# An attention, MLP and mixture-of-experts chain on one core: eight weight conversions moved, and the gates' end interleaved with early expert blocks

## Chip, cores and metric

The kernel runs on one core of one Trainium2 chip. The metric is the device time of one execution in microseconds (us); lower is better.

## What is computed

Three layers follow one another. The output of each is the next one's input.

```python
def _attn_ref(q, k, v, f):                      # 4 batches, 8 heads, 576 positions, 64 wide
    scores = q @ k.T / sqrt(D)                  # per batch and head
    cum = cumsum(log(clip(f, 1e-4, 1)))
    scores = where(causal, -1e9, scores + cum[i] - cum[j])
    return softmax(scores) @ v

def _moe_ref(x, w_in, w_out):                   # 2304 tokens, 512 -> 2048 -> 512
    h = x @ w_in
    return (h * clip(h + 3, 0, 6) / 6) @ w_out

def _moe2_ref(x, w_gate, w_output_gate, w1, w2):   # 8 experts, 512 -> 1024 -> 512
    logits = x @ w_gate
    e_idx = argmax(logits, axis=1)              # one expert for each token
    gate_w = softmax(logits)[e_idx]
    eom = sigmoid(x @ w_output_gate)
    for e in range(8):
        mask = e_idx == e
        out[mask] = gate_w * eom[mask, e] * (relu(x[mask] @ w1[e]) @ w2[e])
```

All of it is float32. The kernel splits each float32 operand into a high half (fp16) and a low half (bf16) and makes each product of three matmuls: high by high, high by low, low by high.

## The kernel before

**Attention** (`attn_seq`) is a long generator of steps: loads and transposes of q, k and v, score matmuls (L295), a softmax on VectorE, ScalarE and GpSimd, and the products with v (L428 to L443). At the end of each group of tokens VectorE scales the result (`xs`, L453), GpSimd makes its low half (`xn`, L457), and SyncE's DMA queue transposes it into `xT` (L491), the input of the MLP.

**The MLP** (`moe1_steps`) takes the 2304 tokens in 6 chunks of 384. A chunk has 16 up-products of 12 matmuls (L695), each evacuated by ScalarE (`hr`, L699) and VectorE (L702) and split (L703, L707), and then 4 down-products of 48 matmuls (L718), evacuated to `x2` (L727, L728). The steps of attention for later tokens are issued between the MLP's steps, so that TensorE has work of both.

**Weight conversion.** `w_in` and `w_out` come as 16 raw tiles each (`load_raw`), and `conv_raw` turns a tile into its halves by a route that keeps the low bits: three integer instructions on VectorE (L658, L660, L662), a copy on ScalarE (L665) and a subtraction (L666) on GpSimd, or on VectorE for two in three of `w_out`'s. `EARLY_CONV` says how many of the 32 tiles are converted among attention's steps before the first chunk; the rest are converted in the first chunk's steps, one for each of its first six steps and then two. Where a conversion is issued in the program is not yet where it runs: a scheduler orders the instructions by priorities, and the conversions in the chunk's steps stand under `high_priority(offset=CONV_FIRST)`, 500, against attention's 200. SP, the engine that issues most loads, has its order by hand there.

**Gates** (`gate_steps(c)`, three parts divided by `yield`). Part one: 36 matmuls (L783) for the logits of a chunk's three token tiles, and the tokens' rows transposed (L791) and stored to DRAM (`rows`, L793, on GpSimd's queue). Part two: a chain on VectorE from `lg` (L797) to the one-hot of the chosen expert (`oh`, L805) and running sums of it (`ohsum`, L809), six small matmuls (L814, L815) that rank each token within its expert (`rank`, L824), the gate's value in three pieces (L816 to L836), and `M` (L837), the values spread over the experts. Gates of chunks 0 to 4 run inside the next chunk's steps. The last chunk's run after its last down-product.

**Count and table.** `count_rounds` counts the tokens of each expert (one matmul, L889, and five VectorE instructions, L892 to L896) for the loop at the end. `rank_onehot` writes `R`, a one-hot of each token's rank (L938). `table` multiplies `R` by `M` (18 token tiles by 2 blocks, 36 matmuls, L916), so that for each slot of each expert it gives the token's row number and gate value (L920 to L929). GpSimd then gathers rows by these numbers (L950), SyncE transposes them into `xs` (L953), and each expert runs `expert1` (8 groups of 12 matmuls, L976, evacuated by ScalarE, L979, and VectorE, L980) and `expert2` (24 matmuls a block, L995, scaled on ScalarE, L1001, and scattered on GpSimd's queue, L1002).

**Early blocks.** The first 128 slots of experts 0 and 1 are filled from the first five chunks' tokens alone, by a table of their own (`R0`, L1126) made during the last chunk. Their `expert1` (`first`, one generator for each, 16 groups in all) and `expert2` run before the main blocks. They read and write room in `wi`, and their sums are in `ps_mm`, a PSUM pool of 3 buffers. From here on the order of PE, ScalarE and VectorE is the program's own (`manual_schedule`):

```python
for g_ in gq:                 # last chunk's gates, all of them
    for _ in g_: pass
count_rounds()
run(first[0], 2)              # two groups of expert 0's early block
rank_onehot x 3; table(R, ...)
rest of first[0], first[1]; expert2 of both; main blocks
```

Of the kernel before, what the change touches and what calls it, by code (L numbers as in the profile page):

```python
# [43 lines left out]

WO_STEP = 12

EARLY_CONV, EARLY_LOADS = 18, 21

PE_PIECES = 4

# [8 lines left out]
def attention_moe_kernel(ctx: ExitStack, tc: tile.TileContext, q, k, v, f, w_in, w_out,  # L59
# [713 lines left out]
    def gate_steps(c):  # L773
# [34 lines left out]
        for i in range(n):  # L808
            nc.vector.tensor_tensor(out=ohsum[:, f0 + i + 1], in0=ohsum[:, f0 + i], in1=oh[:, f0 + i],  # L809
                                    op=ALU.add)  # L810
        pr = ps_mm.tile([P, 512], F32, tag="mm", name="mm")
        for i in range(n):
            o = pr[:, i * E:(i + 1) * E]
# [72 lines left out]
    def count_rounds():  # L886

        ps = ps_mm.tile([P, 512], F32, tag="mm", name="mm")
        nc.tensor.matmul(ps[:, 0:E], lhsT=allone, rhs=ohsum[:, NB], start=True, stop=True)  # L889
        mx = mp2.tile([P, 1], F32, tag="cmx", name="cmx")  # L890
        more = mp2.tile([P, 8], F32, tag="more", name="more")
        nc.vector.tensor_reduce(out=mx, in_=ps[:, 0:E], axis=AX.X, op=ALU.max)  # L892
        nc.vector.tensor_tensor(out=more, in0=mx.to_broadcast([P, 8]), in1=thr, op=ALU.is_gt)
        nc.vector.tensor_reduce(out=mx, in_=more, axis=AX.X, op=ALU.add)
        nc.vector.tensor_copy(out=nrounds, in_=mx)
        nc.vector.tensor_copy(out=cnt, in_=ps[:, 0:E])  # L896
# [40 lines left out]
    def rank_onehot(R, i, s0, s1):  # L937
        nc.vector.tensor_scalar(out=R[:, i], in0=iota[:, s0:s1], scalar1=rank[:, i:i + 1], scalar2=None,  # L938
                                op0=ALU.is_equal)
# [23 lines left out]
    def expert1(e, ps_pool, blocks):  # L963

        W1, (xs, o) = wts[e, 0], xs_t[e, blocks[0]]
        hT, ho = h_t[e, blocks[0]]
        w = len(blocks) * P
        hs = slice(ho, ho + w)
        for m in range(F2 // P):
            ps = ps_pool.tile([P, 512], F32, tag="mm", name="mm")  # L970
            i = 0
            for j in range(KD):
                for a, b2 in ((0, 0), (0, 1), (1, 0)):
                    l = W1[:, a, j, m * P:(m + 1) * P]
                    r = xs[:, b2 * KD + j, o:o + w]
                    nc.tensor.matmul(ps[:, 0:w], lhsT=l.bitcast(BF16) if a else l, rhs=r.bitcast(BF16) if b2 else r,  # L976
                                     start=i == 0, stop=i == 3 * KD - 1)
                    i += 1
            nc.scalar.activation(out=hT[:, m, 0, hs], in_=ps[:, 0:w], func=AF.Relu)  # L979
            nc.vector.scalar_tensor_tensor(out=hT[:, m, 1, hs].bitcast(BF16), in0=ps[:, 0:w], scalar=0.0,  # L980
                                           in1=hT[:, m, 0, hs], op0=ALU.max, op1=ALU.subtract)
            yield
# [93 lines left out]
    for c in range(NCH):  # L1076
# [56 lines left out]
            while len(complete) < need[c + 1]:  # L1133
                adv()
        gq.append(gate_steps(c))
    for g_ in gq:
        for _ in g_:
            pass
    run(wg_, 4 * KD + 1 - nw)
    count_rounds()  # L1140
    ET = mybir.EngineType

    first = [expert1(e, ps_mm, (0,)) for e in range(2)]
    manual = ctx.enter_context(ExitStack())
    manual.enter_context(tc.manual_schedule(engines={ET.PE, ET.Activation, ET.DVE}))
    run(first[0], 2)
    for i in range(NBL, NB):
        rank_onehot(R, i, P, CAP)
    table(R, P, const, ps_mm, (1, 2), NB)
    for g_ in first:  # L1150
        run(g_, F2 // P)
# [2 lines left out]
            pass  # L1154
    moe1_ctx.close()
    xp = ctx.enter_context(tc.tile_pool(name="xp", bufs=1))
    ps2 = ctx.enter_context(tc.tile_pool(name="ps2", bufs=5, space=PSUM))
    regs = []

    def round_(first):  # L1160
# [85 lines left out]
```

## Time and profile before

| | |
|---|---|
| median of 3 runs | 831.59 us (827.8 to 831.8) |
| the profiled execution's own time | 830.41 us |
| its span, first to last instruction | 828.7 us |
| mean granted TensorE clock | 0.964 of full speed |
| TensorE busy (matmuls) | 744.0 us, 90% of the span |
| VectorE, ScalarE, GpSimd busy | 470.3, 449.9, 317.2 us |

The busy shares are means over stages that differ. The stage of attention alone takes the first 70 us or so; attention and the MLP share the engines up to some 580 us; the gates' end, the table and the early blocks lie between 588 and 619 us; the main blocks fill the rest. A row of a timeline gives the start, the duration and the instruction, and in brackets how long its engine stood idle just before it and what ended that.

### The profile page before, as it was taken

Reading aid. Unit: us, or ns where it says so; the run is one execution under the profiler, and the core shown is the slowest. Engines: PE = TensorE matmul, PEld = TensorE weight load, DVE = VectorE, ACT = ScalarE, POOL = GpSimd, SP = SyncE. Lnnn points to the kernel's source line nnn. Section 1 sums busy time; section 2 is a strip of 40 time slices with the busy share of each in tenths; the row PEclk is TensorE's granted clock in tenths of the full one; section 3 lists DMA queues with packets and bytes.
Section 4 is the critical chain, followed back from the end, with each engine's and each line's share of the span. In section 5 each row is a group of like instructions: output and inputs, shape, how many; then the busy total and the mean of one; then the engine's idle time right before and its main releaser. Section 6 shows DMA issues by size and latency. Waiting matters only on the chain.

```text
span 828.7 us, 16710 instructions
## 1 busy us (share of the span) xinstructions
PE 744.0 (90%) x6177; PEld 478.4 (58%) x6177; DVE 470.3 (57%) x1267; ACT 449.9 (54%) x909; POOL 317.2 (38%) x393
## 2 busy tenths in 40 slices
PE   4745989978899999998999999999899999999993
PEld 2533556645655655565665666566668665667641
DVE  7998988547651865158623776760313555554510
ACT  4864789756882775277724654550113545454510
POOL 9546788845753463145522500000131232310010
PEclk9986989989999999998999999999999999999997
DMA  8758799979985783497623847612474899895410
GB/s 248 214 184 192 180 214 257 193 128 167 176 154 116 138 141 74 74 145 143 107 55 67 145 138 238 177 41 51 78 150 94 240 281 267 231 265 200 149 37 29
DMA packets 263778, 127.95 MB, mean 154 GB/s; under 512 B 214658, under 2 KB 247522, under 8 KB 263684
## 3 DMA queue, kind: packets, MB, share of 16 engines
q1 hardware_dynamic: 251860, 105.20, 58.5%
q0 software_dynamic: 4960, 15.73, 5.5%
q10 hardware_dynamic: 6864, 5.80, 2.6%
q8 instruction: 54, 0.88, 0.4%
q14 instruction: 40, 0.33, 0.1%
HBM read 71.52 MB, written 10.08 MB: 98 GB/s over the span
## 4 chain that ended last, share of the span: by engine, by line
PE 38%; DMA 28%; DVE 11%; issue 7%; ACT 7%; POOL 4%; SPq 2%; ACTq 0%; another core or an unknown queue 0%; POOLq 0%; DVEq 0%
PE mm L718 14%; PE mm L695 12%; DMA out_dram<-y,ids 7%; DMA stw<-in_moe_w_dram 4%; DMA xg<-rows,ids 4%; PE mm L976 4%; DMA pt<-pn 3%; PE mm L995 3%; PE sc L295 2%; DMA q<-qp 2%; DMA K<-kp 2%; DVE W L879 1%; ACT ms L376 1%; DMA ldk<-in_k_dram 1%; DVE g L707 1%
## 5 line engine op out<-in xcount | busy, mean ns | idle before, releaser
L695 PE MATMUL mm<-xT,wi 128*128 128x384 f16 (+1 forms) x1152 | 213.3, 335 | 7.5 <-DMA xT<-xn 5.1
L718 PE MATMUL mm<-g,wo 128*128 128x384 f16 (+1 forms) x1152 | 199.8, 326 | 1.9 <-ACT g L703 1.1
L695 PEld LDWEIGHTS <-wi 128*128 128x128 f16 (+1 forms) x1152 | 112.1, 100 | 85.2 <-issue 19.7
L718 PEld LDWEIGHTS <-wo 128*128 128x128 f16 (+1 forms) x1152 | 110.7, 98 | 75.2 <-issue 4.6
L976 PEld LDWEIGHTS <-W 128*128 128x128 f16 (+1 forms) x1344 | 100.6, 99 | 16.2 <-issue 8.0
L879 DVE TENSOR_TENSOR W<-stw,W 128x1024 bf16<-128x1024 f32 x64 | 77.7, 1224 | 52.8 <-ACT W L878 48.8
L376 ACT ACTIVATE ms<-ms,nm 128x512 f32<-128x512 f32 (+4 forms) x144 | 78.8, 576 | 48.5 <-DVE nm L342 27.1
L394 POOL TENSOR_TENSOR pn<-ms,pn 128x384 bf16<-128x384 f32 (+1 forms) x80 | 82.4, 1034 | 57.8 <-ACT pn L393 52.6
L976 PE MATMUL mm<-xs,W 128*128 128x256 f16 (+3 forms) x1152 | 97.1, 246 | 4.7 <-DVE hT L980 2.3
L995 PE MATMUL mm<-W,hT 128*128 128x512 f16 (+1 forms) x432 | 94.4, 379 | 1.0 <-DVE hT L980 0.6
L878 ACT ACTIVATE W<-stw 128x1024 f16<-128x1024 f32 x64 | 66.9, 1054 | 47.7 <-DMA stw<-in_moe_w_dram 45.4
L707 DVE TENSOR_TENSOR g<-hr,g 128x384 bf16<-128x384 f32 x80 | 58.1, 726 | 33.6 <-ACT g L703 33.4
L342 DVE CUSTOM_DVE_ANT_1 ms<-sc,mask 128x128 f32<-128x128 f32 (+3 forms) x128 | 59.2, 486 | 26.1 <-PE sc L295 12.1
L995 PEld LDWEIGHTS <-hT 128*128 128x128 f16 (+1 forms) x432 | 41.9, 98 | 51.3 <-issue 1.9
L702 DVE SCALAR_TENSOR_TENSOR hr<-hr,mm 128x384 f32<-128x384 f32 x96 | 52.7, 549 | 28.1 <-ACT hr L699 27.5
L703 ACT ACTIVATE g<-hr 128x384 f16<-128x384 f32 x96 | 49.4, 515 | 28.0 <-DVE hr L702 27.4
L699 ACT ACTIVATE hr<-mm,bias 128x384 f32<-128x384 f32 x96 | 54.4, 567 | 16.5 <-PE mm L695 14.5
L980 DVE SCALAR_TENSOR_TENSOR hT<-mm,hT 128x128 bf16<-128x128 f32 (+1 forms) x96 | 32.0, 355 | 50.4 <-ACT hT L979 48.1
L428 PE MATMUL pv<-vt,pt 128*128 128x65 f16 x320 | 41.2, 198 | 20.9 <-DVE xs L453 9.4
L1002 POOL DMA_INDIRECT out_dram<-y,ids x18 | 20.7, 1148 | 97.9 <-ACT y L1001 57.2
L295 PE MATMUL sc<-K,q 128*128 128x256 f16 (+3 forms) x192 | 48.7, 296 | 6.4 <-DVE nm L342 4.3
L393 ACT ACTIVATE pn<-ms 128x384 f16<-128x384 f32 (+1 forms) x80 | 44.3, 556 | 13.3 <-DMA pt<-pn 12.9
(189 smaller groups left out, 1113.5 us busy)
## 6 DMA issues: line engine op xcount, KB each, us to landing
stw<-in_moe_w_dram SPq DMA_DIRECT2D x64, 512.0 KB
wo<-in_moe_w_in_dram SPq DMA_DIRECT2D x16, 512.0 KB
raw<-in_moe_w_out_dram ACTq DMA_DIRECT2D x11, 512.0 KB
rows<-rw POOLq DMA_DIRECT2D x15, 256.0 KB, 3.5
ldk<-in_k_dram SPq DMA_DIRECT2D x14, 256.0 KB
ldq<-in_q_dram SPq DMA_DIRECT2D x14, 256.0 KB
ldv<-in_v_dram SPq DMA_DIRECT2D x13, 256.0 KB
g<-in_moe_w_out_dram SPq DMA_DIRECT2D x3, 512.0 KB
```

The source lines that it names most:

```text
L295: nc.tensor.matmul(po, lhsT=lhs[0:rows], rhs=r if n > 1 else r[:, :, 0], start=x == 0, stop=x == 1)
L342: nc.vector.tensor_tensor_reduce(out=pairs(ms[:, off:off + w]), in0=ps[:, 0:w].rearrange("p (c j) -> p c j", c=2), in1=pairs(mask[:, 640 - ...
L376: nc.scalar.activation(out=ms[:, off:off + w], in_=ms[:, off:off + w], func=AF.Exp, scale=-1.0, bias=nm[:, i:i + 1])
L394: nc.gpsimd.tensor_tensor(out=lo.bitcast(BF16), in0=ms[:, 0:N], in1=hi, op=ALU.subtract)
L695: nc.tensor.matmul(ps[:, 0:w], lhsT=l.bitcast(BF16) if a else l, rhs=r.bitcast(BF16) if b2 else r, start=i == 0, stop=i == 3 * KD - 1)
L699: nc.scalar.activation(out=hr, in_=ps[:, 0:w], func=AF.Relu, bias=bias3)
L707: either.tensor_tensor(out=g[:, m, 1, 0:w].bitcast(BF16), in0=hr, in1=g[:, m, 0, 0:w], op=ALU.subtract)
L718: nc.tensor.matmul(ps[:, 0:w], lhsT=l.bitcast(BF16) if a else l, rhs=r.bitcast(BF16) if b2 else r, start=i == 0, stop=i == 3 * NF - 1)
L878: nc.scalar.activation(out=hi, in_=sts[i], func=AF.Copy)
L879: nc.vector.tensor_tensor(out=lo.bitcast(BF16), in0=sts[i], in1=hi, op=ALU.subtract)
L976: nc.tensor.matmul(ps[:, 0:w], lhsT=l.bitcast(BF16) if a else l, rhs=r.bitcast(BF16) if b2 else r, start=i == 0, stop=i == 3 * KD - 1)
L995: nc.tensor.matmul(ps, lhsT=l.bitcast(BF16) if a else l, rhs=r.bitcast(BF16) if b2 else r, start=i == 0, stop=i == 3 * NF2 - 1)
```

## The change

It has two parts.

1. `EARLY_CONV` goes from 18 to 10: eight tiles' conversions (and the room they free for later raw loads) are issued in the first chunk's steps rather than ahead of it.
2. At the gates' end a third `yield` splits part two of `gate_steps` ahead of the ranking matmuls. The last chunk's gates are no longer run as one piece. The order becomes: two groups of the early block; the logits and VectorE's chain up to `ohsum`; three groups; the ranking, the gate's values and `M`; the count; three `R`; three groups of expert 0 and two of expert 1; the table; the remaining six groups; `expert2`. The early blocks' sums go to `ps2`, a pool of 5 PSUM buffers that was opened later before, and the manual order begins earlier.

Lines below L810 are one further down in the changed kernel (L814 is now L815, L976 is L977), and those of the expert stage's caller up to four.

```diff
-EARLY_CONV, EARLY_LOADS = 18, 21
+EARLY_CONV, EARLY_LOADS = 10, 21
...
             nc.vector.tensor_tensor(out=ohsum[:, f0 + i + 1], in0=ohsum[:, f0 + i], in1=oh[:, f0 + i],
                                     op=ALU.add)
+        yield
         pr = ps_mm.tile([P, 512], F32, tag="mm", name="mm")
...
-    for g_ in gq:
-        for _ in g_:
-            pass
     run(wg_, 4 * KD + 1 - nw)
-    count_rounds()
     ET = mybir.EngineType
-
-    first = [expert1(e, ps_mm, (0,)) for e in range(2)]
+    ps2 = ctx.enter_context(tc.tile_pool(name="ps2", bufs=5, space=PSUM))
+
+    first = [expert1(e, ps2, (0,)) for e in range(2)]
     manual = ctx.enter_context(ExitStack())
     manual.enter_context(tc.manual_schedule(engines={ET.PE, ET.Activation, ET.DVE}))
+    last, = gq
     run(first[0], 2)
+    run(last, 2)
+    run(first[0], 3)
+    run(last, 2)
+    count_rounds()
     for i in range(NBL, NB):
         rank_onehot(R, i, P, CAP)
+    run(first[0], 3)
+    run(first[1], 2)
     table(R, P, const, ps_mm, (1, 2), NB)
     for g_ in first:
         run(g_, F2 // P)
...
-    ps2 = ctx.enter_context(tc.tile_pool(name="ps2", bufs=5, space=PSUM))
```

Three places in the engines' orders show what this does. The first is GpSimd (POOL) ahead of the first chunk, where L457 is the low half of attention's result (`xn`) and L666 the low half of a converted weight tile. Before:

```order
L666 TENSOR_TENSOR wi<-w_588,wi 128x4x128
L457 TENSOR_TENSOR xn<-xs,xn 128x128
L666 TENSOR_TENSOR wi<-w_622,wi 128x4x128
L666 TENSOR_TENSOR wi<-w_665,wi 128x4x128
L457 TENSOR_TENSOR xn<-xs,xn 128x128
L666 TENSOR_TENSOR wi<-w_700,wi 128x4x128
```

and with the change:

```order
L666 TENSOR_TENSOR wi<-w_923,wi 128x4x128
L457 TENSOR_TENSOR xn<-xs,xn 128x128
L666 TENSOR_TENSOR wi<-w_948,wi 128x4x128
L457 TENSOR_TENSOR xn<-xs,xn 128x128
L666 TENSOR_TENSOR wi<-w_973,wi 128x4x128
L666 TENSOR_TENSOR wi<-w_1018,wi 128x4x128
```

One conversion now stands between the last two `xn` where two stood. On VectorE likewise 12 conversions instead of 13 are done ahead of the last `xs` (L453) of the first chunk, and 16 instead of 17 ahead of the first `hr` (L702); the others, though written later, are placed by their priority where they were. On TensorE 116 of attention's score matmuls (L295) stand ahead of the first chunk's last up-product, where 129 stood, and 188 in both cases ahead of the second chunk.

The second place is VectorE at the gates' end. L837 (now L838) is the end of the gates' chain, L938 (L939) the table's one-hot `R`, L980 (L981) an early block's evacuation, L920 to L924 (L921 to L925) the table's results. Before:

```order
L836 TENSOR_TENSOR vals<-z,vb 128x3
L980 SCALAR_TENSOR_TENSOR wi<-mm,wi 128x128
L938 TENSOR_SCALAR R<-iota,rank 128x256 x2
L837 TENSOR_TENSOR M<-vals,oh 128x168
L938 TENSOR_SCALAR R<-iota,rank 128x256
L920 COPY sv<-mm 128x112
L922 SCALAR_TENSOR_TENSOR u<-sv 128x16
L924 CAST ids<-u 128x16
```

and with the change:

```order
L838 TENSOR_TENSOR M<-vals,oh 128x168
L893 TENSOR_REDUCE cmx<-mm 128x1
L894 TENSOR_TENSOR more<-cmx,thr 128x8
L895 TENSOR_REDUCE cmx<-more 128x1
L896 CAST nrounds<-cmx 128x1
L897 CAST cnt<-mm 128x8
L939 TENSOR_SCALAR R<-iota,rank 128x256 x3
L981 SCALAR_TENSOR_TENSOR wi<-mm,wi 128x128 x5
L921 COPY sv<-mm 128x112
L923 SCALAR_TENSOR_TENSOR u<-sv 128x16
L925 CAST ids<-u 128x16
```

The count has moved behind `M`, and five evacuations stand ahead of the table's results. The third place is ScalarE in the same stretch; L727 is the last evacuation of the MLP, L807 and L820 (L821) the gates' exponentials, L979 (L980) the early blocks' evacuations. Before:

```order
L727 ACTIVATE x_7847<-mm 128x3x128 x4
L807 ACTIVATE t_8051<-t_8051 128x24
L820 ACTIVATE z<-z 128x3
L979 ACTIVATE wi<-mm 128x128 x16
L1001 ACTIVATE wi<-mm,cf 128x512 x2
```

and with the change:

```order
L727 ACTIVATE x_7847<-mm 128x3x128 x4
L980 ACTIVATE wi<-mm 128x128 x2
L807 ACTIVATE t_8086<-t_8086 128x24
L980 ACTIVATE wi<-mm 128x128 x3
L821 ACTIVATE z<-z 128x3
L980 ACTIVATE wi<-mm 128x128 x11
L1002 ACTIVATE wi<-mm,cf 128x512 x2
```

Five evacuations now lie among the gates' exponentials. On TensorE the stretch was 36 matmuls of L783, 6 of L814 and L815, 1 of L889, 24 of L976, 36 of the table (L916), 168 of L976, 48 of L995. Now it is 24 of the early block, the 36 of the gates, 36 of the early block, the 7 small ones, 60 of the early blocks, the 36 of the table, 72 of the early blocks, and the 48.

## Rows read from the trace of the kernel before

**Rows 1.** Busy time of PE, PEld, DVE, ACT, POOL in one stretch; clock, DMA share, GB/s.

```profile
100.00:150.00 50.00, 45.59 (x374) 29.25 (x374) 43.85 (x123) 44.61 (x94) 42.92 (x49) 0.93 1.12 227
```

**Rows 2.** Groups by line, one group: shapes, count, busy us, mean ns, idle before.

```profile
L658 DVE TENSOR_SCALAR cv<-raw 128x512 int32<-128x512 int32 x13 | 9.0, 691 | 4.2 <-DMA raw<-in_moe_w_out_dram 4.1
```

**Rows 3.** Timeline of VectorE before the first chunk: start us, us, instruction.

```profile
67.26 0.69 DVE L662 SCALAR_TENSOR_TENSOR w<-wo,cv 128x512 int32<-128x512 int32 x1
67.86 0.28 DVE L453 TENSOR_TENSOR xs<-pv,rl 128x128 f32<-128x128 f32 x1
```

**Rows 4.** Timeline of GpSimd, the same stretch; in brackets the idle time before.

```profile
68.69 1.16 POOL L666 TENSOR_TENSOR wi<-w,wi 128x512 bf16<-128x512 f32 x1 [1.13 <-ACT wi L665]
69.80 0.43 POOL L457 TENSOR_TENSOR xn<-xs,xn 128x128 bf16<-128x128 f32 x1
```

**Rows 5.** Timeline of TensorE: the first chunk's first matmuls.

```profile
73.44 5.96 PE L695 MATMUL mm<-xT,wi 128*128 128x384 f16 x26 [3.63 <-DMA xT<-xn]
```

**Rows 6.** Timeline of TensorE: first chunk's last up-product, second chunk's first.

```profile
125.17 2.11 PE L695 MATMUL mm<-xT,wi 128*128 128x384 f16 x12
...
177.57 2.72 PE L695 MATMUL mm<-xT,wi 128*128 128x384 f16 x8 [1.49 <-DMA xT<-xn]
```

**Rows 7.** Timeline of TensorE: gates, table, early blocks, first main block.

```profile
588.33 0.37 PE L783 MATMUL mm<-wg,x 128*128 128x16 f16 x9
...
589.67 0.79 PE L783 MATMUL mm<-wg,x 128*128 128x16 f16 x25 [0.39 <-DVE x L728]
591.84 0.18 PE L814 MATMUL mm<-oh,tri 128*128 128x8 f16 x1 [1.38 <-DVE oh L805]
...
592.53 2.72 PE L976 MATMUL mm<-wi,W 128*128 128x128 f16 x24
595.04 0.77 PE L916 MATMUL mm<-M,R 128*128 128x56 bf16 x15
596.57 0.86 PE L916 MATMUL mm<-M,R 128*128 128x56 bf16 x21 [0.77 <-DVE M L837]
...
603.07 0.83 PE L976 MATMUL mm<-wi,W 128*128 128x128 f16 x12 [0.22 <-DVE wi L980]
605.26 3.51 PE L976 MATMUL mm<-wi,W 128*128 128x128 f16 x60 [1.36 <-DVE wi L980]
608.61 10.52 PE L995 MATMUL mm<-W,wi 128*128 128x512 f16 x48
618.97 3.51 PE L976 MATMUL mm<-xs,W 128*128 128x128 f16 x60
```

**Rows 8.** Busy time and granted clock of short stretches there, columns as in group 1.

```profile
590.00:592.00 2.00, 0.62 (x22) 0.52 (x19) 1.40 (x11) 0.22 (x1) 0.00 (x0) 1.00 1.48 73
592.00:594.00 2.00, 1.96 (x22) 1.71 (x20) 1.67 (x17) 0.20 (x1) 0.00 (x0) 0.52 0.56 117
594.00:596.00 2.00, 1.81 (x27) 1.69 (x25) 1.00 (x7) 0.55 (x2) 0.69 (x2) 0.62 1.07 202
...
604.00:606.00 2.00, 0.74 (x14) 0.73 (x14) 0.69 (x3) 0.62 (x3) 0.00 (x0) 1.00 0.69 163
```

**Rows 9.** Timeline of ScalarE: evacuations of the early blocks.

```profile
604.61 0.62 ACT L979 ACTIVATE wi<-mm 128x128 f16<-128x128 f32 x3 [1.92 <-PE mm L976]
```

**Rows 10.** Timeline of VectorE: start of the gates' chain, row numbers of the table.

```profile
590.50 0.21 DVE L797 COPY lg<-mm 128x48 f32<-128x48 f32 x1 [0.88 <-PE mm L783]
...
598.00 0.18 DVE L924 CAST ids<-u 128x16 uint32<-128x16 f32 x1
```

**Rows 11.** Timeline of GpSimd: store of the rows, gathers of the main blocks.

```profile
597.08 0.54 POOL L793 DMA_DIRECT2D rows<-wi  x1 [0.60 <-DMA wi<-x]
600.32 0.99 POOL L950 DMA_INDIRECT xg<-rows,ids  x1 [2.70 <-PE mm L976]
...
609.21 0.94 POOL L950 DMA_INDIRECT xg<-rows,ids  x1 [5.37 <-DMA xs<-xg]
```

**Rows 12.** TensorE's waits from 640 us to the end: us, times, longest.

```profile
PE mm L976 <- DVE hT L980: 1.8, 2, 1.4
```

## Prediction, made before the changed kernel ran

> **What bounds the kernel now.** I read the table of busy time first: TensorE is busy in 90% of the span, so a gain has to be found where TensorE waits or runs slowly. I then went through TensorE's idle time by stretch. In the early stretch, where attention shares the engines with the first chunk, TensorE has 45.59 us of matmuls in 50 us, VectorE 43.85, ScalarE 44.61 and GpSimd 42.92 [rows 1]: four engines are nearly full, and a delay on any of them can come out on TensorE. After the main blocks begin there is almost nothing left: the largest wait of the tail is 1.8 us in all [rows 12]. Between lies the gates' end, and here the timeline of TensorE shows what the second part of the change is about [rows 7]. From the first gate matmul (588.33) to the first main block (618.97) go 30.64 us, with gaps of 1.38 us for the gates' one-hot, 0.77 for `M`, 0.22 and 1.36 for evacuations. The table of short stretches adds that TensorE was busy for only 0.62 of the 2 us from 590, and that in the 4 us after that the granted clock was 0.52 and 0.62 [rows 8], the lower of the two levels (1.2 of 2.4 GHz) for most of the time. So the emptiness is paid twice, as gaps and as slow matmuls right behind them.
>
> **Part B, the gates' end.** No work is added or removed; it is put in another order. I rebuild TensorE's time from its own rows at full clock [rows 7]. An early-block matmul costs 0.0585 us (60 in 3.51). Then: two groups, 24 matmuls, 1.40; the 36 gate matmuls at the pace of the 25 that ran in 0.79, 1.14; three groups, 2.11; seven small matmuls, 0.69 (591.84 to 592.53); five groups, 3.51; the table, 36 at the pace of 21 in 0.86, 1.47; six groups, 4.21; `expert2`, 10.36 (608.61 to 618.97). Together 24.9 us against 30.64.
>
> Which gaps stay? The wait for the last evacuations of `x2` goes, as 1.40 us of other matmuls stand there. The wait for the one-hot (1.38) is covered by three groups (2.11): the chain begins when the gates' logits are done, some 0.4 us later than 590.50 [rows 10], and needed 1.3 us to the first ranking matmul. The wait for `M` came 6.1 us after the chain's start (590.50 to 596.57) [rows 7, 10]; in the new order the table stands 588.33 + 1.40 + 1.14 + 2.11 + 0.69 + 3.51 = 597.2, behind a chain that starts at 590.9 and has two evacuations fewer in it, but now the count's five instructions and all three `R` lie between `M` and the table's last matmuls. I bound this wait by 0 and by the 0.77 of before, and take 0.5: the chain is as long as before, with a little more behind it. So 25.4 us, a gain of 5.2.
>
> The evacuations (0.22 and 1.36) are less sure. On ScalarE one came after an idle 1.92 us behind a matmul [rows 9], at a pace that the three-buffer pool alone does not explain, as there were no other instructions between. If the cause is the small pool, five buffers remove it. If it is something that these rows do not show, it returns. The bounds of the gain are therefore 5.7 (no wait for the table) and 5.2 - 1.6 = 3.6. **I take 5.0**, nearer to the upper end, because the row that waits is TensorE's own, for a buffer to come free, and the order gives it two more.
>
> What is delayed? Five evacuations stand ahead of the table's results, and the count ahead of that, so the row numbers (598.00 before [rows 10]) come later, by my estimate at about 599.6: the table's last matmul at 597.2 + 1.5 + 0.5, and VectorE's copy and two more steps. The gather that needs them started only at 600.32, 3.2 us behind the store of the last rows at 597.08 [rows 11]; the releaser that the row names, a matmul, has no part in it, and the store is what it must wait for. So there is room of 0.7 us. Behind it there is more: the GpSimd queue's gather at 609.21 had waited 5.37 us for the transposed rows of an earlier one [rows 11], so the first main rows were in place by then, 9.8 us before TensorE came to them at 618.97. If TensorE comes 5.0 us sooner, 4.8 us of slack are left. The count, now later, is read on ScalarE only after the early blocks' `expert2`. I charge nothing for either.
>
> The clock: with matmuls in place of the gap nothing in the new order looks like 590 to 592. If it fell all the same, the price is read from the 24 matmuls that took 2.51 us (592.53 to 595.04) instead of 1.40, so 1.1 us. The Trainium skill has a rule that speaks against the new order ("TensorE: Matmul & The Clock Gate", section "A second HAM failure mode: psum-queue depth-cycling"): where groups of matmuls cycle through PSUM buffers and TensorE idles a little between groups, the clock goes down and up and the throughput suffers. The early blocks now cycle through five buffers beside VectorE's chain, and by that rule the gain would be about 3.9 us rather than 5.0. The trace doesn't bear it out: from 604 to 606, with a busy time of 0.74 us in 2 between two such groups, the clock was 1.00 [rows 8]. That result is inside the forecast's range below and gets no chance of its own.
>
> **Part A, eight conversions.** Written later, but their priority pulls them forward: on VectorE the order hardly changes (12 conversions instead of 13 ahead of the first chunk's last `xs`, 16 instead of 17 ahead of its first evacuation). The work is the same: three VectorE instructions of 0.69 us a tile [rows 2]. What does change is GpSimd. Before, a conversion's subtraction ran from 68.69 for 1.16 us and held back the last `xn`, which was ready when `xs` ended at 68.14 (67.86 + 0.28) [rows 3, 4]. `xn` ran at 69.80, its transpose followed, and TensorE, idle for 3.63 us, began the first chunk at 73.44 [rows 5]. With one subtraction fewer ahead, `xn` can start 69.80 - 68.14 = 1.7 us sooner, so the first chunk at about 71.7. Against it: one conversion, 3 x 0.69 = 2.1 us of VectorE, moves to where the engine is 88% busy [rows 1]. As it had 6.15 us of idle time in these 50, I charge a third, 0.7. **I take a gain of 1.0**, between 1.8 (another 0.1 from an earlier `xs`) and a loss of 2.1. The waits for raw tiles (4.1 us of VectorE [rows 2]) hang on a loop of two buffers and stay.
>
> **The sum.** 830.41 - 5.0 - 1.0 = 824.4 us for an execution like the profiled one. That one lies 1.2 us under the median of 831.59, so a median would be 825.6; between the two I say 825.0. A measurement of this kernel can tell some 0.5%, 4.2 us, from no change: faster means under 827.4, slower over 835.7.
>
> **Rivals.**
> 1. *The early reshuffle gives 3 to 5 us back.* The first chunk's order changes on all engines. For it: four engines nearly full [rows 1]. Against: the work is the same, and the second chunk finds the same number of score matmuls ahead of it. 824.4 + 3 to 5, with the median's distance: 828 to 831, no change.
> 2. *Attention falls behind, slower.* At the first chunk's last up-product, 13 of attention's score matmuls that were done before are still to come (116 instead of 129). If they aren't caught up beside the down-products, the second chunk waits for its `xT`: from 125.17 to its start at 177.57 [rows 6] attention advanced by 59 of these matmuls, 0.89 us each, so 13 cost 11.5 us. That would give 830.4 + 11.5 - 5.0 = 836.9. It decides once the second chunk's first matmul comes over some 10 us later than 177.57. Against it: at 177.57 TensorE had idled for only 1.49 us [rows 6], and the order restores the count before the second chunk.
> 3. *The gathers come late.* If the table's row numbers slip so far that the main rows land over 4.8 us later than before, TensorE waits at the first main block instead, and at 9.8 us the whole gain of B is gone: 829.4, no change. Against it: the 1.6 us that I find.
> 4. *Both at their good ends*, and VectorE's raw waits gone with earlier loads: 830.4 - 5.7 - 1.8 - 4.1 = 818.8 us, say 818.5. Against it: TensorE does not wait for the raw loads themselves.
> 5. *The change does not move the conversions at all* would make A 0.0: 825.4. It is inside the forecast.
>
> **How the numbers follow.** Forecast 0.55, with its own range 820.5 to 829 (A from -1.8 to +2.1, B from 3.6 to 5.7, the median or the profiled time as base); 0.50 of it lies under 827.4 and 0.05 above. Rival 1: 0.21. Rival 2: 0.07. Rival 3: 0.07. Rival 4: 0.10. Faster 0.50 + 0.10 = 0.60; same 0.05 + 0.21 + 0.07 = 0.33; slower 0.07. The range runs from 818 to 832: it holds the forecast and rivals 1, 3 and 4 and leaves out rival 2 and the ends of the unknown costs.
>
> **What the changed profile would show.** Part B is right if between the first gate matmul and the `expert2` of the early blocks no gap over 0.8 us is left, the granted clock stays near 1.00 in all stretches from 588 to 600, and the first main block starts some 25 us behind the last down-product instead of 30.6. It is wrong if a gap in front of the table over 1 us names `M` or `R`, if the evacuations again stall by 1 us or more on five buffers, or if the first main block waits for `xs`. Part A is right if the first chunk starts near 71.7 with a gap of about 2 us, and wrong if `xn` is again held. The second chunk's start against 177.57 settles rivals 1 and 2: up to 176 my forecast, 178 to 181 rival 1, over 187 rival 2. The prediction fails as a whole if the last down-product of the last chunk ends later than the 588.3 of before by more than 3 us.

## The result, and the profile after

The changed kernel's median was 820.92 us (819.37 to 826.54, 6 runs) against 831.38 us (827.8 to 831.8, 6 runs) for the kernel before: ratio 0.9901, 95% interval 0.9876 to 0.9927. In a second measurement, beside the experiments below, the ratio was 0.9927 (0.989 to 0.9965). The predicted median was 825.0 in a range of 818 to 832, with faster at 0.6: direction and size held. The gain forecast for part A did not come, and a part of the gain was not foreseen.

The profiled execution is the slowest of the six, 826.54 us, with a span of 824.8 us, and its early part comes later than in a second profile of the same kernel (818.25 us), which is used beside it. The gates' end is the same in both. This is the timeline of TensorE of the changed kernel there, the rows that answer to [rows 7]:

```profile
590.85 1.50 PE L977 MATMUL mm<-wi,W 128*128 128x128 f16 x24
592.19 1.05 PE L783 MATMUL mm<-wg,x 128*128 128x16 f16 x36
593.10 2.17 PE L977 MATMUL mm<-wi,W 128*128 128x128 f16 x36
595.10 0.17 PE L815 MATMUL mm<-oh,tri 128*128 128x8 f16 x1
...
595.28 3.51 PE L977 MATMUL mm<-wi,W 128*128 128x128 f16 x60
598.63 0.55 PE L917 MATMUL mm<-M,R 128*128 128x56 bf16 x15
599.44 1.06 PE L917 MATMUL mm<-M,R 128*128 128x56 bf16 x21 [0.26 <-DVE R L939]
600.34 4.18 PE L977 MATMUL mm<-wi,W 128*128 128x128 f16 x72
604.36 10.52 PE L996 MATMUL mm<-W,wi 128*128 128x512 f16 x47
615.41 3.12 PE L977 MATMUL mm<-xs,W 128*128 128x128 f16 x53 [0.53 <-issue]
```

From the last down-product (590.85) to the first main block (615.41) it takes 24.56 us, where it took 30.64. No gap is left but 0.26 us in front of the table, for `R`, and 0.53 in front of the main block. The clock held, as the table of short stretches shows (columns as in [rows 8]: PE, PEld, DVE, ACT, POOL, clock, DMA share, GB/s):

```profile
592.00:594.00 2.00, 2.00 (x60) 2.00 (x58) 1.24 (x7) 0.28 (x1) 0.00 (x0) 1.00 0.34 68
594.00:596.00 2.00, 2.00 (x43) 2.00 (x41) 1.84 (x11) 0.83 (x4) 0.35 (x1) 1.00 1.02 191
...
604.00:606.00 2.00, 1.95 (x17) 1.14 (x16) 0.58 (x2) 0.44 (x2) 1.41 (x2) 1.00 0.04 10
```

All three stand at 1.00, where 0.52 and 0.62 were granted from 592 to 596. VectorE's and GpSimd's rows tell what became late. VectorE first:

```profile
593.28 0.21 DVE L797 COPY lg<-mm 128x48 f32<-128x48 f32 x1 [0.29 <-PE mm L783]
...
598.12 0.33 DVE L838 TENSOR_TENSOR M<-vals,oh 128x168 bf16<-128x168 f32 x1
...
599.11 0.67 DVE L939 TENSOR_SCALAR R<-iota,rank 128x256 f16<-128x256 f16 x3
...
601.19 0.17 DVE L925 CAST ids<-u 128x16 uint32<-128x16 f32 x1
```

`M` is done 5.2 us after the chain's start, and `R` follows behind the count. The row numbers come at 601.19, 10.3 us behind the last down-product, where they came 9.7 us behind it (588.33 to 598.00). Then GpSimd's queue:

```profile
601.03 0.54 POOL L793 DMA_DIRECT2D rows<-wi  x1 [3.44 <-DMA wi<-x]
604.28 0.99 POOL L951 DMA_INDIRECT xg<-rows,ids  x1 [2.71 <-ACT wi L980]
...
613.35 0.94 POOL L951 DMA_INDIRECT xg<-rows,ids  x1 [5.53 <-DMA xs<-xg]
```

The first gather again starts 3.2 us behind the store of the last rows (601.03 to 604.28). The gather at 613.35, which waits for the first transposed main rows, comes only 2.1 us ahead of TensorE's first main block; it was 9.8 us ahead before [rows 7, 11]. What made the first gather later is not the row numbers, which were there 3.1 us ahead of it, but that store: it waited 3.44 us for its transposed rows, 0.60 before [rows 11]. The gathers are likely the next bound, and may act already: in the six profiles of this order on five buffers the main block starts 11.1 to 11.6 us after the first gather, in five of them behind a gap of 0.29 to 0.64 us for which the profile names no cause; in all others it starts 12.7 us or more after it, without a gap. In the early part, the two starts of chunks that the prediction named:

```profile
73.68 2.72 PE L695 MATMUL mm<-xT,wi 128*128 128x384 f16 x8 [2.46 <-DMA xT<-xn]
...
184.92 5.33 PE L695 MATMUL mm<-xT,wi 128*128 128x384 f16 x17 [1.29 <-DMA xT<-xn]
```

The first chunk starts 0.2 us later than before [rows 5], not 1.7 sooner; the second starts 7.4 us later than before [rows 6]. In the second profile of the same kernel the two are 71.87 and 179.10.

### The profile page after: what moved, and what is told of

It is laid out like the page before. It is cut to its first block, busy times and chain, and to the rows that moved or that the text cites. A ratio compares the mean times of both kernels' runs of the same rounds, so it can differ in the third digit from the quotient of the medians.

```text
span 824.8 us, 16716 instructions
## 1 busy us (share of the span) xinstructions
PE 741.9 (90%) x6166; PEld 478.2 (58%) x6177; DVE 465.2 (56%) x1267; ACT 451.1 (55%) x909; POOL 319.3 (39%) x393
## 4 chain that ended last, share of the span: by engine, by line
PE 47%; DMA 26%; DVE 8%; issue 7%; ACT 6%; POOL 3%; SPq 1%; POOLq 0%; ACTq 0%; DVEq 0%
PE mm L718 21%; PE mm L695 11%; DMA out_dram<-y,ids 8%; DMA xg<-rows,ids 4%; PE mm L996 4%; PE mm L977 4%; DMA pt<-pn 4%; PE sc L295 3%; DMA K<-kp 2%; ACT ms L376 1%; DMA stw<-in_moe_w_dram 1%; DMA xT<-xn 1%; DVE ms L342 1%; POOL pn L394 1%; DMA ldv<-in_v_dram 1%
## 5 line engine op out<-in xcount | busy, mean ns | idle before, releaser
L977 PEld LDWEIGHTS <-W 128*128 128x128 f16 (+1 forms) x1344 | 99.5, 98 | 15.3 <-issue 7.9
L394 POOL TENSOR_TENSOR pn<-ms,pn 128x384 bf16<-128x384 f32 (+1 forms) x80 | 81.8, 1026 | 63.2 <-ACT pn L393 55.5
L977 PE MATMUL mm<-xs,W 128*128 128x256 f16 (+3 forms) x1152 | 97.0, 246 | 5.6 <-DVE hT L981 2.6
L707 DVE TENSOR_TENSOR g<-hr,g 128x384 bf16<-128x384 f32 x80 | 54.9, 688 | 33.1 <-ACT g L703 33.0
L702 DVE SCALAR_TENSOR_TENSOR hr<-hr,mm 128x384 f32<-128x384 f32 x96 | 52.7, 549 | 30.0 <-ACT hr L699 29.4
L703 ACT ACTIVATE g<-hr 128x384 f16<-128x384 f32 x96 | 49.2, 516 | 28.7 <-DVE hr L702 28.5
L981 DVE SCALAR_TENSOR_TENSOR hT<-mm,hT 128x128 bf16<-128x128 f32 (+1 forms) x96 | 31.8, 353 | 53.2 <-ACT hT L980 37.6
L295 PE MATMUL sc<-K,q 128*128 128x128 f16 (+3 forms) x192 | 48.8, 298 | 9.6 <-DVE nm L342 6.1
L428 PE MATMUL pv<-vt,pt 128*128 128x65 f16 x320 | 41.5, 197 | 17.6 <-DVE xs L453 10.2
```

The lines of the kernel that those rows point to most:

```text
L295: nc.tensor.matmul(po, lhsT=lhs[0:rows], rhs=r if n > 1 else r[:, :, 0], start=x == 0, stop=x == 1)
L394: nc.gpsimd.tensor_tensor(out=lo.bitcast(BF16), in0=ms[:, 0:N], in1=hi, op=ALU.subtract)
L707: either.tensor_tensor(out=g[:, m, 1, 0:w].bitcast(BF16), in0=hr, in1=g[:, m, 0, 0:w], op=ALU.subtract)
```

## The experiments

Each ratio is to runs of the kernel before in the same session. "The stretch" is the time from the last down-product to the first main block.

**1. Part B alone**, and **2. part A alone.** The edits are the change's own, one part at a time:

```diff
-EARLY_CONV, EARLY_LOADS = 10, 21
+EARLY_CONV, EARLY_LOADS = 18, 21      # e1: the changed kernel, with 18
-EARLY_CONV, EARLY_LOADS = 18, 21
+EARLY_CONV, EARLY_LOADS = 10, 21      # e2: the kernel before, with 10
```

> Part B alone: eighteen tiles are converted ahead of the first chunk as before, the gates' end is in the new order. Theory 1 (the parts add, B is worth what the stretch from the last down-product to the first main block lost in the two profiles, 30.6 - 24.6 = 6.1 us): 831.4 - 6.1 = 825.3 us, and that stretch at 24.6 us again. Theory 2 (B is worth more than its stretch, because the tail behind it gains as well, and A nothing): near 821, with a shorter time from the first main block to the end. Rival (B's gain is given back in the tail): over 828.

> Part A alone: ten tiles are converted ahead of the first chunk, the gates' end is as before. Theory 1 (what the medians leave after B, 10.5 - 6.1 = 4.4 us, is A's): 827 us, the last down-product ending some 4 us sooner than 588.3. Theory 2 (A is worth nothing or a little loss, as the profiled run of the changed kernel shows, whose last down-product ended 2.5 us later): 831 to 834. My prediction said 1.0 us of gain: 830.4.

Part B alone: 819.92 us against 826.83, ratio 0.9907 (0.9873 to 0.9941), with the stretch at 24.32 us. Part A alone: 830.48 us, ratio 1.0039 (1.0019 to 1.0060), so slower by 3.2 us. B is all of the gain, and theory 1's 6.1 us lies within its interval (4.9 to 10.5). A alone is a cost; theory 2 had the direction, as "nothing or a little loss".

**3. The changed kernel once more.**

> The changed kernel once more, to see on the same chip how its executions spread and what a second profile of it looks like. Theory 1 (the spread of 819.4 to 826.5 comes from the early stretch, where attention and the first chunks share four nearly full engines): the stretch from the last down-product to the first main block is 24.6 us again, and the second chunk's start differs from 184.92 by about as much as the whole time differs from 826.5. Rival (the spread comes from the tail): the second chunk starts at 184 to 186 and the last down-product ends near 590.9 whatever the whole time.

819.62 us, ratio 0.9927 (0.989 to 0.9965). The stretch is 24.60 us again. The profiled execution was 818.25 us, 8.3 us under the first profile; the second chunk starts 5.8 us sooner, the last down-product ends 5.1 us sooner (585.75), and the rest of the difference lies behind the first main block (206.2 us to the end of the span instead of 209.4). So the spread comes mostly from the early stretch, not only from it.

**4. Three buffers** for the early blocks in the new order, with eighteen early conversions.

```diff
-    first = [expert1(e, ps2, (0,)) for e in range(2)]
+    first = [expert1(e, ps_mm, (0,)) for e in range(2)]
```

> Part B alone, with the early blocks' sums in the pool of three PSUM buffers that the gates and the table use, instead of the five buffers of their own. Theory 1 (the order alone fills the gaps, buffers matter little): within 1 us of part B alone. Rival (five buffers are what the order needs, as five evacuations stand behind M, the count and R on VectorE): groups 6 to 10 wait for VectorE in front of the table, 2 to 3 us more than part B alone, and the clock falls again behind that gap.

820.75 us, ratio 0.993 (0.9905 to 0.9956), which the timing can't tell from 0.9907. The profile can: the stretch is 25.89 us, and TensorE's timeline shows why.

```profile
590.98 1.50 PE L977 MATMUL mm<-wi,W 128*128 128x128 f16 x24
594.27 2.29 PE L977 MATMUL mm<-wi,W 128*128 128x128 f16 x36 [1.79 <-DVE cnt L897]
```

```profile
592.00:594.00 2.00, 0.48 (x9) 0.36 (x7) 1.72 (x12) 0.40 (x2) 0.68 (x2) 1.00 0.85 281
594.00:596.00 2.00, 1.73 (x29) 1.65 (x29) 1.49 (x8) 0.35 (x2) 0.42 (x1) 1.00 0.43 160
```

After 24 of the 60 matmuls TensorE waits 1.79 us until VectorE has read out the count's own sum (L897), which holds the buffer that the third group needs. The rival was right about the wait: the stretch is 1.6 us longer than in experiment 1, instead of 2 to 3. It was wrong about the clock, which stayed at 1.00, though TensorE worked for only 0.48 of the 2 us from 592 (the short stretches above).

**5. Five buffers alone**, in the old order.

```diff
-    first = [expert1(e, ps_mm, (0,)) for e in range(2)]
+    ps2 = ctx.enter_context(tc.tile_pool(name="ps2", bufs=5, space=PSUM))
+    first = [expert1(e, ps2, (0,)) for e in range(2)]
```

> The kernel before with one edit: the early blocks' sums go to five PSUM buffers of their own. The gates' end keeps its old order, eighteen tiles are converted early. Theory 1 (the order fills the gaps, the buffers matter only once evacuations stand behind M and R): the stretch from the last down-product to the first main block stays at 28.5 to 30.6 us, the time within 1 us of before. Rival (the stalls of 0.22 and 1.36 us before the fifteenth and sixteenth groups come from a pool of three): the stretch falls to about 28.7 us without those stalls, 1.6 to 2 us faster than before.

828.02 us against 829.39, ratio 0.9987 (0.9959 to 1.0015): no difference. With its own pool the planner moved the two early groups up among the gates' matmuls, so `M` was waited for longer (2.06 us, 0.77 before [rows 7]). TensorE's timeline, then the table of short stretches:

```profile
597.18 1.14 PE L916 MATMUL mm<-M,R 128*128 128x56 bf16 x21 [2.06 <-DVE M L837]
598.14 11.71 PE L976 MATMUL mm<-wi,W 128*128 128x128 f16 x168
```

```profile
592.00:594.00 2.00, 0.61 (x25) 0.52 (x22) 1.59 (x12) 0.43 (x2) 0.00 (x0) 1.00 0.69 130
...
598.00:600.00 2.00, 2.00 (x25) 2.00 (x23) 1.43 (x9) 0.28 (x1) 0.54 (x1) 0.50 0.55 211
```

That longer wait alone does not explain the low clock. TensorE had worked for only 0.61 us from 592 to 594, while it waited for the gates' one-hot, as before [rows 8]; behind that it was granted 0.91 and then, from 596 on, 0.50, and the 168 matmuls take 11.71 us. In the two profiles of part A alone, one kernel with three buffers and waits for `M` of 0.69 and 0.62 us, the same 168 took 9.59 us (experiment 2) and 11.72 us (experiment 12):

```profile
595.77 9.59 PE L976 MATMUL mm<-wi,W 128*128 128x128 f16 x168
...
603.69 11.72 PE L976 MATMUL mm<-wi,W 128*128 128x128 f16 x168
```

The stretch is 28.73 and 31.25 us there, and 29.89 us here: in the old order, how long the clock stays low differs from one execution to the next.

**6 and 7. Two early conversions.**

```diff
-EARLY_CONV, EARLY_LOADS = 18, 21
+EARLY_CONV, EARLY_LOADS = 2, 21       # e6: in the kernel before; e7: in the changed one
```

> Twice the move of part A on the kernel before: two tiles converted ahead of the first chunk instead of eighteen (the change: ten). Theory 1 (the priority places the conversions where they were, so A is worth nothing that repeats, and the 0.4% of part A alone is a shift of an order that nothing in it explains): within 2 us of before. Rival (A truly costs, as conversions slip behind attention's and the first chunk's work): 4 to 7 us slower than before, with the first chunk's up-products waiting for wi.

> The changed kernel with two early conversions instead of ten. Theory 1 (A is nothing, B is all): the time of part B alone, 6 to 7 us under before. Rival (A costs by itself): 2 to 4 us above part B alone, so only 3 to 4 us under before.

1135.78 us and 1122.8 us, and they answer nothing about A. Three of `w_out`'s raw tiles are loaded into the room of `g`, the up-products' results. With two early conversions the first chunk's ninth up-product writes there before those tiles are converted, so that the rest of the kernel works on other weights; 264 of the 300 us more of experiment 6 are TensorE's busy time: 2688 matmuls of the main blocks' `expert1` instead of 1152, a further pass of the loop at the end. By the program's order this begins below nine early conversions, so ten is almost as far as the move can go; that limit is read from the program, and no value between was tried.

**8. No groups between the count and the table.** The kernel of experiment 1 without `run(first[0], 3)` and `run(first[1], 2)` ahead of the table.

> Part B alone without the five groups between the count and the table: two groups, the logits, three groups, ranking and M, count, three R, table, the other eleven. Theory 1 (those groups cover the wait for M and R): TensorE waits in front of the table's last matmuls from about the end of the small matmuls, 3.5 us less the 0.6 us of the table's first fifteen plus the 0.26 us that are left now, some 3 us, and the clock may fall behind that gap, which adds 1 to 1.4 us: 3 to 4.5 us slower than part B alone. Rival (M is ready sooner where nothing else stands on VectorE): a wait of 1 us or less, within 1 us of part B alone.

824.18 us, ratio 0.993 (0.9903 to 0.9957). TensorE's timeline and the short stretches:

```profile
590.83 0.55 PE L917 MATMUL mm<-M,R 128*128 128x56 bf16 x15
595.00 1.46 PE L917 MATMUL mm<-M,R 128*128 128x56 bf16 x21 [3.62 <-DVE R L939]
```

```profile
592.00:594.00 2.00, 0.00 (x0) 0.00 (x0) 1.76 (x13) 0.00 (x0) 0.57 (x1) 1.00 0.90 241
...
596.00:598.00 2.00, 2.00 (x27) 2.00 (x25) 1.30 (x8) 0.22 (x1) 0.00 (x0) 0.50 0.08 27
```

The wait for `R` is 3.62 us, TensorE does nothing from 592 to 594, and the clock is 0.50 from 596 to 598. The stretch is 29.39 us, 5.1 us more than with those groups (24.32). In the stretch theory 1 held, a little over its size; by time the two ratios differ by 1.9 us only, with intervals that overlap. A puzzle was left: this kernel gains only about 1.1 us in its stretch against the old order's 30.5 (mean of four profiles), and yet was 5.8 us faster than before by its ratio. So something outside the gates' end is faster too.

**What was found in the traces.** The kernels with the new `yield` differ from the others most clearly at one place in the middle. In the kernel before, 371 us, VectorE, GpSimd and TensorE:

```profile
371.55 4.34 DVE L707 TENSOR_TENSOR g<-hr,g 128x384 bf16<-128x384 f32 x1 [2.68 <-ACT g L703]
375.81 0.57 DVE L469 TENSOR_SCALAR xs<-pv,rl 64x64 f32<-64x64 f32 x2
...
370.54 0.56 POOL L793 DMA_DIRECT2D rows<-rw  x1 [4.72 <-DMA rw<-x]
371.12 1.17 POOL L215 TENSOR_TENSOR kp<-ldk,kp 64x512 f16<-64x512 f32 x1
372.23 0.91 POOL L394 TENSOR_TENSOR pn<-ms,pn 128x384 bf16<-128x384 f32 x1
373.10 1.12 POOL L318 TENSOR_TENSOR vt<-ldv,vt 128x512 bf16<-128x512 f32 x1
374.19 0.42 POOL L457 TENSOR_TENSOR xn<-xs,xn 128x128 bf16<-128x128 f32 x1
374.57 0.90 POOL L394 TENSOR_TENSOR pn<-ms,pn 128x384 bf16<-128x384 f32 x1
...
376.53 0.19 PE L428 MATMUL pv<-vt,pt 128*128 128x65 f16 x1 [4.74 <-DVE xs L469]
```

L707 reads two tensors and takes 4.34 us where the median of its 80 is 0.56. It ends (375.89) just behind five GpSimd instructions that run back to back to 375.47, lined up behind a store of the gates' rows (L793) for which GpSimd's queue had stood idle for 4.72 us, and the scaling L469 behind it keeps TensorE waiting for 4.74 us. The Trainium skill has the rule ("SBUF — State Buffer", section "Who interferes with whom"): an instruction of VectorE with two inputs in SBUF and one of GpSimd that reads SBUF share a port, and the one that comes second is blocked until the first is done. These rows agree, with the addition that the block lasted through five GpSimd instructions; that the port is the cause is read from this overlap, and no run tested it alone. The long L707 (4.30 to 4.69 us) is in five of the six profiles in which the middle gates stand as before, and in none of the seven with the `yield` there at the seventh step. In the sixth, of experiment 6, the same five GpSimd instructions and one more ran back to back from 386.07 to 390.81, and it was another two-input instruction that was held, while one with a single input just ahead of it was not. VectorE there:

```profile
386.47 0.18 DVE L804 TENSOR_REDUCE cm<-t 128x3 f32<-128x24 f32 x1
386.68 4.17 DVE L805 TENSOR_TENSOR oh<-t,cm 128x24 f16<-128x24 f32 x1
```

The store that they lined up behind waited 4.6 to 4.9 us in these six profiles, and 1.1 to 1.8 in the seven; why is not shown. The `yield` cuts `gate_steps` for every chunk: for the first five, the loop runs one part at its steps 3, 5 and 7, so the ranking and `M` moved from step 5 to step 7, where nothing was left to run before.

**9. The yield alone**, and **10. the end alone.**

```diff
             nc.vector.tensor_tensor(out=ohsum[:, f0 + i + 1], in0=ohsum[:, f0 + i], in1=oh[:, f0 + i],
                                     op=ALU.add)
+        yield                                  # e9: the kernel before with this line
...
-                run(gq[0])
+                run(gq[0], 2 if k_ == 5 else 1)   # e10: the kernel of e1 with this line
```

> The kernel before with the new yield in gate_steps and nothing else. The gates of the first five chunks run one part at the third, fifth and seventh step of the next chunk, so the new yield moves their ranking matmuls, their gate values and M from the fifth step to the seventh; the last chunk's gates are run whole, as before. Theory 1 (the yield alone is worth something in the middle of the kernel, which I did not see when I predicted): 3 to 5 us faster than before; the VectorE instruction of 4.3 us near 371 us that is in all three profiles with the old gates (an L707 that otherwise takes 0.55) and the TensorE wait of 4.7 us behind it are gone; the gates' end takes 28.7 to 30.6 us. Rival (the yield moves small work only, all of B is the gates' end): within 1 us of before.

> Part B's new order at the gates' end, with the middle gates as before: at the fifth step two parts are run, so that ranking and M stay there. Eighteen tiles are converted early. Theory 1 (the end and the middle add): 3 to 5 us faster than before, the stretch from the last down-product to the first main block at 24.6 us, the L707 of 4.3 us and the wait of 4.7 us near 371 back. Rival (all of B is the end): 6 to 7 us faster than before, as part B alone.

The yield alone: 825.46 us against 830.29, ratio 0.9955 (0.9927 to 0.9983), 3.7 us. The end alone: 823.23 us, ratio 0.9922 (0.9892 to 0.9953), 6.5 us. VectorE's longest instruction at that place and TensorE's wait, first with the yield alone, then with the end alone:

```profile
367.97 2.14 DVE L802 TENSOR_TENSOR t<-lg,mx 128x24 f32<-128x24 f32 x1
...
371.47 0.19 PE L428 MATMUL pv<-vt,pt 128*128 128x65 f16 x1 [0.24 <-DVE xs L469]
...
378.40 0.17 PE L815 MATMUL mm<-oh,tri 128*128 128x8 f16 x1 [1.57 <-DVE hr L702]
```

```profile
369.55 4.36 DVE L707 TENSOR_TENSOR g<-hr,g 128x384 bf16<-128x384 f32 x1 [2.87 <-ACT g L703]
...
374.54 0.21 PE L428 MATMUL pv<-vt,pt 128*128 128x65 f16 x1 [4.84 <-DVE xs L469]
```

With the yield alone nothing there takes over 2.2 us and the wait of 4.7 us is 0.24; a new one of 1.57 stands in front of the ranking. With the end alone the old pair is back, at 4.36 and 4.84 us, while the stretch is 24.40 us. The gains add within their intervals: 3.7 + 6.5 = 10.2 against 7.7 (4.9 to 10.5) for both in experiment 1. By time alone the end has the rival's 6 to 7 us; that it is not all of B rests on experiment 9 and on the rows. The profiles as a whole agree: from the second chunk's start to the last down-product it is 411.0 us in the mean of five profiles with the old middle (409.5 to 413.7) and 407.6 in the mean of six with the `yield` at the seventh step (405.9 to 412.4, the last in experiment 1; experiments 6 and 7 are left out).

**11. The ranking at step nine**, in the changed kernel.

```diff
-            if gq and k_ in (3, 5, 7):
+            if gq and k_ in (3, 5, 9):
                 run(gq[0])
-                if k_ == 7:
+                if k_ == 9:
```

> The changed kernel with the middle gates' last part moved on, from the seventh to the ninth step. Theory 1 (at the seventh step the ranking matmuls come before VectorE has finished the running sums, behind the first evacuations of the chunk: TensorE waits 1.2 to 2.0 us for that in the profiles with the yield): these waits are gone, and the time is 1 to 2 us under the changed kernel's, 8 to 9 us under before. Rival (what moves meets other work there): the changed kernel's 7 us under before, or less.

831.07 us, ratio 1.001 (0.998 to 1.004): all of the gain is gone, some 7 to 9 us. The rival held, and by more than it said. The stretch is still 24.67 us; the loss lies ahead of it, with 415.3 us from the second chunk's start to the last down-product. TensorE's waits from 180 to 588 us, in the changed kernel of experiment 3 and here (us, times, longest):

```profile
PE mm L695 <- DVE hr L702: 2.0, 1, 2.0
...
PE mm L815 <- DVE hr L702: 1.2, 1, 1.2
```

```profile
PE mm L695 <- DVE hr L702: 6.5, 5, 3.1
...
PE mm L718 <- DVE hr L702: 2.4, 1, 2.4
```

The waits in front of the ranking did go. But VectorE is late with the up-products' evacuations (6.5 us in five waits, after 2.0 in one). What exactly it was late with was not tried.

**12. Part A alone, again.**

> Part A alone once more. Theory 1 (its 0.4% was the spread of a program whose early order is sensitive to small shifts; with part B it cost nothing): within 2 us of before. Rival (it costs by itself): again 2.5 to 4.5 us slower.

832.84 us against 830.29, ratio 1.0031 (1.0000 to 1.0062), 2.6 us slower: the rival held, at its lower end. Twice now, so the cost of A alone is real, at about 3 us. Where it arises is seen in the profiles. With ten early conversions the second chunk starts at 180.7 us in the mean of five profiles (177.3 to 184.9), with eighteen at 178.1 in the mean of seven (177.0 to 180.0), a difference of 2.6. And TensorE has a wait that is missing with eighteen. Its waits, and those of SP's queue, from 74 to 185 us, here with A alone (experiment 2), then with B alone:

```profile
PE pv L440 <- DMA pt<-pn: 2.6, 1, 2.6
...
SPq L405 <- POOL pn L394: 10.1, 6, 5.6
```

```profile
SPq L405 <- POOL pn L394: 4.2, 5, 1.9
```

SP's queue waits up to 5.6 us for `pn` of GpSimd before it can transpose it to `pt` (L405); with eighteen early conversions its longest wait for the same instruction (L394) is 1.5 to 2.0 us, and for another write of `pn` (L401) 1.7 to 2.4. TensorE then waits for `pt` in front of L440: 1.6 to 3.7 us in all five profiles with ten, none in six of the seven with eighteen (0.7 in the other). That A costs is shown; that this wait is the cost is only likely, since no run removed it alone. With two early conversions (experiments 6 and 7) it is 0.2 us, and the second chunk comes later still, at 193.6 and 193.0, so more than this wait decides when it starts.

## Why the prediction was right, and where it was not

**Part B at the gates' end: right in mechanism and nearly in size.** The working gave 25.4 us for the stretch and a gain of 5.2, of which I took 5.0. The stretch was 24.3 to 24.7 us in the five profiles with the change's order (experiment 7 left out), against 28.7 to 31.6 (mean 30.5) in four with the old one, so 6.0 us; the end alone was worth 6.5 by time. The terms that were off partly cancel: the seven small matmuls took 0.18 us (595.10 to 595.28) instead of 0.69, the gates' 36 took 0.91 instead of 1.14, the wait in front of the table was 0.26 instead of the 0.5 I charged, and `expert2` with the gap behind it took 11.05 (604.36 to 615.41) instead of 10.36. The gates' chain has three evacuations in it where it had two, not two fewer as I wrote; from `lg` to the end of `M` it is shorter all the same (5.2 us instead of 6.0), with the count and two `R` moved behind it. The slow clock's 1.1 us, which the gain contains, is gone as expected. It is not a fixed price: in the old order the clock stayed low for longer in some executions (experiment 5), and so the mean gain is above the 5.2 worked out from one. Experiment 8 shows that gap and slow clock return together when the covering groups are taken away, experiment 4 that a gap need not bring the slow clock. The Trainium skill's rule on cycling through PSUM buffers ("TensorE: Matmul & The Clock Gate", section "A second HAM failure mode: psum-queue depth-cycling"), by which 1.1 us would have been lost, did not act: the clock was 1.00 throughout this stretch, even with three buffers.

**The stall of the evacuations.** I took it for a matter of three buffers and kept 3.6 as the lower end. In the old order it was in the profile of before (1.36 us) but not in that of experiment 2, where the same 168 matmuls ran in 9.59 us without a gap on three buffers. It comes in some executions only, and what caused it stays open. It was not what five buffers are for: they take the five groups issued ahead of the table, whose sums VectorE reads out only behind `M`, the count and `R` (1.6 us in experiment 4).

**What was delayed: right that it costs little, wrong on what is late and on how much room is left.** I put the row numbers 1.6 us later; against the last down-product they came 0.7 later. The first gather came 1.4 later (12.0 to 13.4 us), with the store of the last rows, a delay that I had put at nothing. Of the slack of 4.8 us that I expected, 2.1 were left, and the 0.53 us in front of the main block may be a part of the cost.

**Part A: wrong.** The step that failed is "`xn` can start 69.80 - 68.14 = 1.7 us sooner, so the first chunk at about 71.7". In the profiled execution `xn` did start 1.4 us sooner (68.37), but its transpose was issued only 0.8 sooner and landed no sooner: the first chunk starts at 73.2 us in the mean with ten and with eighteen. And the 0.7 that I charged against it, for a conversion on VectorE, was too small and probably on the wrong engine: the second chunk starts 2.6 us later in the mean, with new waits for `pn` of GpSimd. The sign of A was wrong: +2.6 and +3.2 us in place of -1.0. Rival 1, the early reshuffle, came nearest to this, at 3 to 5 us, with a chance of 0.21. Rival 2's mark of over 187 was not reached, though the profiled execution came near it with 184.92.

**A part that I did not see.** The prediction treats the `yield` as a cut in the last chunk's gates alone. It cuts all six, and the five in the middle gained 3.7 us by it. I had compared the orders at the gates' end and before the first two chunks, not between. That the total came out is partly luck, for the two errors nearly cancel: 5.0 + 1.0 = 6.0 us predicted; by the single parts 6.5 + 3.7 - 2.9 = 7.3 us, and 8.2 and 6.0 us by the two ratios of the whole. The range was kept for the right reason in its largest term only.

No version that beat the changed kernel clearly came out: part B with eighteen early conversions has 819.92 us beside 819.62 us for the change in the same session, so A's 3 us do not show there. By their ratios, 0.9907 and 0.9927, the change is 1.7 us behind, less than the intervals; whether A costs anything beside B stays open.

## What to carry to other kernels

Where an engine waits on a short chain of another, put independent work there that is as long as the chain, and count the buffers it needs: the results that wait to be read out behind the chain are what sets their number. A gap on TensorE can be paid a second time by a slow clock behind it (1.1 us for 24 matmuls in the profile before), though not each time (experiment 4), so look at the granted clock behind each gap. And when an edit touches a function that is stepped through by a loop, go through every call of it: here one `yield`, meant for the last chunk, was worth 3.7 us in the middle of the kernel.

## What the runs showed of the hardware

A VectorE instruction with two inputs, L707, took 4.30 to 4.69 us instead of 0.56 in five profiles of four kernels, each time while the same five GpSimd instructions ran back to back, and it ended 0.4 us behind the last of them; in a sixth profile L805, with two inputs too, took 4.17 us there, and L804, with one, 0.18. Behind a stretch in which TensorE worked for 0.61 us in 2 (experiment 5), or not at all (experiment 8), the granted clock fell to 0.50, the lower of its two levels (1.2 of 2.4 GHz), and stayed there for a time with TensorE fully busy (2.00 of 2.00 us from 598 to 600 in experiment 5); behind one with 0.48 us in 2 it stayed at 1.00 (experiment 4). And the early part of one and the same program moved by 5.8 us between two executions (second chunk at 184.92 and 179.10), so that single profiles of two kernels can't be compared there.
